# Moving the last x^T phi(k) products: one behind each query product, instead of two in a row at tile 15

## The chip, the cores and the metric

The kernel runs on one core of a Trainium2 chip. The metric is the device time of one execution in microseconds (us), as the median of several runs. TensorE (PE in the profile) does the matmuls, VectorE (DVE) and ScalarE (ACT) take results out of PSUM, GpSimd (POOL) does some elementwise work in SBUF. A profile also gives a span, which is some 1.7 us shorter than the time.

## The reference, cut to what matters

```python
def reference(A_x, A_wqkv, A_wo, B_x, B_w1, B_w3, B_w2, gate_w):
    # x: 2048 tokens x 512, bf16
    g = sigmoid((x * gate_w).sum(-1, keepdims=True))
    # A: linear attention, 32 heads of 16
    phi = lambda t: where(t > 0, t + 1, exp(t)) + 1e-6
    pq, pk = phi(q), phi(k)                       # q, k, v = x @ wqkv
    kv = einsum("bhsd,bhse->bhde", pk, v)         # sum over all tokens
    z  = einsum("bhsd->bhd", pk)                  # sum over all tokens
    a  = (pq . kv / (pq . z + 1e-6)) @ wo
    # B: SwiGLU
    b  = (silu(x @ w1) * (x @ w3)) @ w2
    return g * a + (1 - g) * b
```

The kernel never forms v. It accumulates XP = x^T phi(k), 512 x 512, over the 16 token tiles of 128 tokens (tiles 0 to 15) and gets kv from wv^T XP afterwards. So phase one is: for each tile a product k = x wk, phi(k), and the XP products of an earlier tile. After it come the query products q of the first block of four tiles, the two "remainder" products (the last columns of w1, w3 and the gate), the kv products (kvT), and then the long feed-forward part.

## The kernel before: the parts that matter

phi takes ScalarE once and VectorE twice:

```python
    def phi(dst, ps):
        e_ins = nc.scalar.activation(out=e[:], in_=ps, func=ACT.Exp)
        nc.vector.tensor_scalar(                       # L142, "the min step", bf16 in SBUF
            out=em[:], in0=e[:], scalar1=1.0, scalar2=1e-6, op0=ALU.min, op1=ALU.add)
        nc.vector.scalar_tensor_tensor(                # L145, reads PSUM, writes phi
            out=dst, in0=ps, scalar=0.0, in1=em[:], op0=ALU.max, op1=ALU.add)
```

GpSimd adds up phi(k) of each tile for z (`pks`, L194), and splits the sum into two bf16 parts at the end (`pks_hi` L423, `pks_lo` L425):

```python
    def emit_k_phi(k_ps, t):
        e_ins = phi(pk_sb[:, t, :], k_ps[:])
        ... # t == 0: a copy
            nc.gpsimd.tensor_add(pks[:], pks[:], pk_sb[:, t, :])
```

The XP products of tile t are four matmuls of 128x512 into four PSUM banks. k, q, the remainder products (`emit_rem`) and the feed-forward products share four other banks in turn (pool `psM`), so a product needs the bank that the fourth product before it used.

The order of the PE instructions is that of the program text. The order of the other engines' instructions is set by the scheduler of the framework, and each engine then runs its own list in that order. The order at the end of phase one, before:

```python
    for t in range(TPB, NT):                                   # TPB = 4, NT = 16
        for u in range(n_xp, n_xp + (2 if t in (NT - 4, NT - 1) else 1)):
            emit_xp(u, XP_ps)
            n_xp = u + 1
        emit_k(t)
    emit_q(0, 0, psM, "mm")
    emit_xp(NT - 2, XP_ps)
    emit_q(0, 1, psM, "mm")
    emit_xp(NT - 1, XP_ps)
    for dc in range(KC):                     # the four "XP casts", PSUM to SBUF
        if dc % 2 == 0:
            nc.scalar.activation(out=XP_sb[:, dc, :], in_=XP_ps[dc][:], func=ACT.Copy)
        else:
            nc.vector.tensor_copy(out=XP_sb[:, dc, :], in_=XP_ps[dc][:])
    emit_q(0, 2, psM, "mm")
    emit_q(0, 3, psM, "mm")
    emit_rem(0, 0, psM, "mm")
    emit_rem(0, 1, psM, "mm")
    ... # kvT: reads XP_sb, then the feed-forward part
```

I write k13 for the k product of tile 13, XP13 for its XP products, q0 to q3 for the query products. On PE the order is: k13 XP11 k14 XP12 XP13 k15 q0 XP14 q1 XP15 q2 q3 rem0 rem1 kvT.

## Time and profile before

| | before |
|---|---|
| time, median of the first 3 runs | 180.62 us (180.34 to 180.81) |
| span of the profiled run | 178.7 us |
| PE busy | 174.9 us, 98% |
| granted clock of PE | full in every slice |
| pair of XP products at tile 12 (XP8 and XP9) | 1.73 us |
| pair of XP products at tile 15 (XP12 and XP13) | 1.80 us |

The page, head and the two rows of slices for PE (40 equal slices of the span; a digit is the busy share, or the granted clock, in tenths):

```profile
span 178.7 us, 2488 instructions
PE 174.9 (98%) x893; PEld 84.6 (47%) x893; DVE 118.2 (66%) x205; ACT 66.6 (37%) x126; POOL 61.4 (34%) x69
...
PE   8999999999999999999999999999999999999993
PEclk9999999999999999999999999999999999999999
```

PE is the bound, but its busy share hides small holes, because the ends of matmuls are modelled and overlap the next start: one 128x512 matmul shows 379 ns, but a group of four takes only 0.86 us, 216 ns each. The chain of waits (start, length, what) has a step for each group of matmuls and shows a hole as an overlong step. Here is the chain of before at the end of phase one:

```profile
22.90 1.73 PE XP L204 x8
...
26.36 0.86 PE k_ps L184 x4
27.22 0.86 PE XP L204 x4
28.08 0.86 PE k_ps L184 x4
28.95 1.80 PE XP L204 x8
30.74 0.86 PE k_ps L184 x4
...
35.06 1.73 PE q_ps L217 x8
36.79 1.36 PE r_ps L241 x16
38.15 0.89 PE kvT_ps L413 x16
39.04 0.86 PE gate_ps L310 x4
39.91 0.86 PE up_ps L318 x4
```

Four full matmuls take 0.86 us. Eight take 1.73 us at tile 12 and 1.80 us at tile 15: that 0.07 us is the only irregular step in this stretch. The timeline of all engines (start, length, engine, line, what, idle time before it) shows what it waited for:

```profile
27.64 1.16 POOL L194 TENSOR_TENSOR pks<-pks,pk_sb 128x512 f32<-128x512 f32 x1 [1.02 <-DVE pk_sb L145]
27.89 1.05 DVE L142 TENSOR_SCALAR phi_m<-phi_e 128x512 bf16<-128x512 bf16 x1 [0.39 <-ACT phi_e L140]
...
28.78 1.96 PE L204 MATMUL XP<-pk_sb,x_sb 128*128 128x512 bf16 x8
28.98 0.69 DVE L145 SCALAR_TENSOR_TENSOR pk_sb<-k_ps,phi_m 128x512 bf16<-128x512 f32 x1
...
29.72 0.53 PEld L204 LDWEIGHTS <-x_sb 128*128 128x128 bf16 x3 [0.19 <-issue]
...
35.27 0.28 DVE L142 TENSOR_SCALAR phi_m<-phi_e 128x512 bf16<-128x512 bf16 x1
35.35 1.22 POOL L425 TENSOR_TENSOR pks_lo<-pks,pks_hi 128x512 bf16<-128x512 f32 x1
```

phi of tile 13 is done at 28.98 + 0.69 = 29.67 us; XP13 would have come up at 28.78 + 0.86 = 29.64 us. (From the end of VectorE's work to the start of the matmul that needs it some 0.04 us more pass.) The profile names nothing that the weight loads waited for before 29.72 ("issue"). The min step of tile 13 took 1.05 us, while GpSimd's addition was running. Where it meets no earlier GpSimd instruction it takes 0.28 or 0.29 us, as at 29.61 us for tile 14; the min steps of tiles 11 and 12 met additions too, and took 1.02 and 0.61 us.

### The profile page before, as it was taken

The page shows a single profiled execution, that of the slowest core. Times are in us where ns is not written, and L with a number is a line of the kernel's source. Part 1 is how long each engine was busy: PE and PEld are TensorE (multiplying, and loading weights), DVE is VectorE, ACT ScalarE, POOL GpSimd, SP SyncE. Part 2 cuts the span into 40 slices and gives each one's busy share as a digit, 9 for nine tenths or more (in the row PEclk, how much of TensorE's full clock was granted, in tenths as well). Part 3 has the DMA queues.
Part 4 walks back from the last instruction along what each step waited for, and adds up shares of the span by engine and source line. Part 5 has one row for each costly group of instructions (what it writes and reads, how often), then busy time and mean ns, then how long its engine had stood idle before and what let it go on. Part 6 is the DMA issues. An engine that isn't in the chain of part 4 may idle for free.

```text
span 178.7 us, 2488 instructions
## 1 busy us (share of the span) xinstructions
PE 174.9 (98%) x893; PEld 84.6 (47%) x893; DVE 118.2 (66%) x205; ACT 66.6 (37%) x126; POOL 61.4 (34%) x69
## 2 busy tenths in 40 slices
PE   8999999999999999999999999999999999999993
PEld 3544444474444545444444544444545444444463
DVE  0588867696998837398786375978754669776000
ACT  3642322666533333342433333342433323341221
POOL 5187575646353323262003232620032328100000
PEclk9999999999999999999999999999999999999999
DMA  6999999601005010124000111240001023300011
GB/s 177 265 280 290 298 362 355 216 0 28 9 11 108 0 48 29 44 54 93 0 4 6 38 37 37 59 93 2 0 7 58 15 62 64 61 0 0 29 44 50
DMA packets 29085, 14.88 MB, mean 83 GB/s; under 512 B 19632, under 2 KB 28816, under 8 KB 29072
## 3 DMA queue, kind: packets, MB, share of 16 engines
q1 hardware_dynamic: 28800, 14.46, 29.5%
q10 hardware_dynamic: 272, 0.26, 0.5%
q8 instruction: 7, 0.11, 0.3%
q14 instruction: 6, 0.05, 0.1%
HBM read 8.42 MB, written 2.10 MB: 59 GB/s over the span
## 4 chain that ended last, share of the span: by engine, by line
PE 98%; DVE 0%; issue 0%; DVEq 0%
PE o_ps L355 19%; PE up_ps L318 19%; PE gate_ps L310 19%; PE XP L204 8%; PE o_ps L346 8%; PE q_ps L217 8%; PE k_ps L184 6%; PE r_ps L241 3%; PE k L184 2%; PE o_ps L350 2%; PE warm L161 2%; PE xTp L174 1%; PE kvT_ps L413 1%; PE W_ps L440 0%; DVE o_out L364 0%; PE z_ps L431 0%
## 5 line engine op out<-in xcount | busy, mean ns | idle before, releaser
L318 PE MATMUL up_ps<-xT,w_sb 128*128 128x512 bf16 x160 | 41.1, 379 | 0.0
L310 PE MATMUL gate_ps<-xT,w_sb 128*128 128x512 bf16 x160 | 41.1, 379 | 0.0
L225 POOL TENSOR_TENSOR qz<-pq,z_sb 128x512 f32<-128x512 bf16 x16 | 18.5, 1164 | 60.3 <-DVE pq L145 58.4
L323 ACT ACTIVATE th<-gate_ps 128x512 bf16<-128x512 f32 x40 | 23.9, 597 | 38.1 <-PE gate_ps L310 37.7
L355 PE MATMUL o_ps<-w_sb,hT 128*128 128x512 bf16 (+2 forms) x180 | 37.5, 355 | 0.0
L325 DVE SCALAR_TENSOR_TENSOR gs<-th,gate_ps 128x512 bf16<-128x512 bf16 x40 | 27.4, 684 | 5.8 <-ACT th L323 5.5
L328 DVE TENSOR_TENSOR hT<-up_ps,gs 128x512 bf16<-128x512 f32 x40 | 27.6, 691 | 3.8
L142 DVE TENSOR_SCALAR phi_m<-phi_e 128x512 bf16<-128x512 bf16 x32 | 14.1, 440 | 19.8 <-ACT phi_e L140 19.7
L355 PEld LDWEIGHTS <-hT 128*128 128x128 bf16 x180 | 16.8, 98 | 17.9
L318 PEld LDWEIGHTS <-w_sb 128*128 128x128 bf16 x160 | 15.6, 98 | 18.9
L310 PEld LDWEIGHTS <-w_sb 128*128 128x128 bf16 x160 | 15.6, 98 | 18.7
L360 ACT ACTIVATE o_out<-o_ps,omg 128x512 bf16<-128x512 f32 (+2 forms) x17 | 11.2, 656 | 30.4 <-PE o_ps L355 30.4
L290 POOL TENSOR_TENSOR pqn<-pq,rden 128x512 bf16<-128x512 bf16 x16 | 16.6, 1056 | 14.0 <-DVE rden L283 11.7
L194 POOL TENSOR_TENSOR pks<-pks,pk_sb 128x512 f32<-128x512 f32 x15 | 17.3, 1155 | 8.3 <-DVE pk_sb L145 7.8
L228 DVE TENSOR_REDUCE den<-qz 128x32 f32<-128x512 f32 x16 | 11.0, 685 | 9.0 <-POOL qz L225 8.9
L346 PE MATMUL o_ps<-W_sb,pqT 128*128 128x512 bf16 (+2 forms) x72 | 16.8, 355 | 0.0
L217 PE MATMUL q_ps<-wq_sb,xT 128*128 128x512 bf16 x64 | 16.3, 379 | 0.0
L204 PE MATMUL XP<-pk_sb,x_sb 128*128 128x512 bf16 x64 | 16.2, 379 | 0.0
L140 ACT ACTIVATE phi_e<-k_ps 128x512 bf16<-128x512 f32 x12 | 7.2, 597 | 15.4 <-PE k_ps L184 13.1
L184 PE MATMUL k_ps<-wk_sb,xT 128*128 128x512 bf16 x48 | 12.3, 379 | 0.0
L140 ACT ACTIVATE phi_e<-q_ps 128x512 bf16<-128x512 f32 x16 | 9.6, 597 | 7.0 <-PE q_ps L217 5.8
L145 DVE SCALAR_TENSOR_TENSOR pq<-q_ps,phi_m 128x512 bf16<-128x512 f32 x16 | 11.1, 691 | 0.5
(59 smaller groups left out, 119.3 us busy)
## 6 DMA issues: line engine op xcount, KB each, us to landing
w_sb<-in_B_w_dram SPq DMA_DIRECT2D x6, 640.0 KB, 8.6
out_dram<-o_out SPq DMA_DIRECT2D x15, 128.0 KB, 1.7
x_sb<-in_A_x_dram SPq DMA_DIRECT2D x3, 512.0 KB, 4.0
x_sb<-in_A_x_dram SPq DMA_DIRECT2D x2, 256.0 KB, 3.7
wq_sb<-in_A_wqkv_dram SPq DMA_DIRECT2D x1, 512.0 KB, 5.1
wv_sb<-in_A_wqkv_dram SPq DMA_DIRECT2D x1, 512.0 KB, 6.8
wo_sb<-in_A_wo_dram SPq DMA_DIRECT2D x1, 512.0 KB, 10.0
wk_sb<-in_A_wqkv_dram ACTq DMA_DIRECT2D x1, 256.0 KB, 3.8
```

Source lines behind the costliest of these rows:

```text
L184: nc.tensor.matmul(k_ps[:], lhsT=xT[:, kc, t * P : (t + 1) * P], rhs=wk_sb[:, kc, :], start=(kc == 0), stop=(kc == KC - 1),)
L194: nc.gpsimd.tensor_add(pks[:], pks[:], pk_sb[:, t, :])
L204: nc.tensor.matmul(XP_ps[dc][:], lhsT=x_sb[:, t, dc * P : (dc + 1) * P], rhs=pk_sb[:, t, :], start=(t == 0), stop=(t == NT - 1),)
L217: nc.tensor.matmul(q_ps[:], lhsT=xT[:, kc, ts_tok], rhs=wq_sb[:, kc, :], start=(kc == 0), stop=(kc == KC - 1),)
L225: nc.gpsimd.tensor_tensor(out=qz[:], in0=st[tb, "pq"][:, tt, :], in1=z_sb[:], op=ALU.mult)
L310: nc.tensor.matmul(gate_ps[:], lhsT=w1_sb[:, kc, fsl], rhs=xT[:, kc, tok_sl], start=(kc == 0), stop=(kc == KC - 1),)
L318: nc.tensor.matmul(up_ps[:], lhsT=w3_sb[:, kc, fsl], rhs=xT[:, kc, tok_sl], start=(kc == 0), stop=(kc == KC - 1),)
L323: nc.scalar.activation(out=th[:], in_=gate_ps[:], func=ACT.Tanh, scale=0.5)
L325: nc.vector.scalar_tensor_tensor(out=gs[:], in0=th[:], scalar=1.0, in1=gate_ps[:], op0=ALU.add, op1=ALU.mult)
L328: nc.vector.tensor_tensor(out=st[tb, "hT"][:, fc, :], in0=up_ps[:], in1=gs[:], op=ALU.mult)
L346: nc.tensor.matmul(o_ps[:], lhsT=st[tb, "pqT"][:, c, tsl], rhs=W_sb[:, c, a:b], start=(c == 0), stop=False,)
L355: nc.tensor.matmul(o_ps[:], lhsT=st[tb, "hT"][:, fc, tsl], rhs=w2_sb[:, fc, a:b], start=False, stop=(fc == FC - 1),)
```

## The change

The intent: do not run XP12 and XP13 in a row at tile 15, but give each of the last three tiles' XP products a query product in front of it, so that phi of the tile has time to finish.

```diff
     for t in range(TPB, NT):
-        for u in range(n_xp, n_xp + (2 if t in (NT - 4, NT - 1) else 1)):
+        for u in range(n_xp, n_xp + (2 if t == NT - 4 else 1)):
             emit_xp(u, XP_ps)
             n_xp = u + 1
         emit_k(t)
-    emit_q(0, 0, psM, "mm")
-    emit_xp(NT - 2, XP_ps)
-    emit_q(0, 1, psM, "mm")
-    emit_xp(NT - 1, XP_ps)
+    for tt in range(TPB - 1):
+        emit_q(0, tt, psM, "mm")
+        emit_xp(n_xp + tt, XP_ps)
     ... # the four XP casts, unchanged
-    emit_q(0, 2, psM, "mm")
-    emit_q(0, 3, psM, "mm")
+    emit_q(0, TPB - 1, psM, "mm")
```

The PE order becomes: k13 XP11 k14 XP12 k15 q0 XP13 q1 XP14 q2 XP15 q3 rem0 rem1 kvT. Two things happen: the pair is parted, and XP13 to XP15, with the casts behind the last, move one product later, so k15 and q0 to q2 come one product earlier.

## The prediction

> **What bounds the kernel.** The tensor engine (PE) alone. The page gives PE 98% of a 178.7 us span at full granted clock in every slice; the chain of waits is 98% PE, and the groups table shows no idle time before any of its large matmul groups. As the Trainium skill warns (page "Perfetto Trace Analysis", section "Identifying the Most-Contended Engine"), busy share is a poor measure for PE, since modelled ends overlap: one 128x512 matmul shows 379 ns. So I use the steps of the chain: every four such matmuls take 0.86 us, 216 ns each, the fully streamed rate that the skill's page "TensorE: Matmul & The Clock Gate" gives (section "Back-to-back issue gap"). A change that leaves the matmuls as they are can win only where this stream has a hole.
>
> **What the change removes, adds, moves.** Nothing is added or removed: 64 XP matmuls and 16 of the first block's query matmuls before and after. Only PE order changes. Before: XP12 XP13 k15 q0 XP14 q1 XP15 q2 q3. After: XP12 k15 q0 XP13 q1 XP14 q2 XP15 q3.
>
> **The hole.** The chain shows the pair of XP products at tile 12 taking 1.73 us (full rate) and the pair at tile 15 taking 1.80 us. In the timeline, phi(k) of tile 13 is finished on VectorE at 28.98 + 0.69 = 29.67 us, while XP13 could start at about 28.78 + 0.86 = 29.64 us; weight loads show one idle time of 0.19 us just before 29.72. So the pair loses 0.07 us to phi(k13): its min step on VectorE took 1.05 us instead of 0.29, beside GpSimd's addition of the previous tile. With k15 and q0 in between, XP13 starts near 31.4, 1.7 us after its operand. That hole goes: -0.07 us, all on the critical path.
>
> **What moves against it.** XP15 ends 0.8 us later, so the four XP evacuations end at about 37.0 instead of 36.16 us. Their reader, kvT, started at 37.99, now about 37.92: margin falls from about 1.8 to about 0.9 us. q2 and its phi now compete with those casts on VectorE. Work there from 35 to 39 us is about 4.1 us (three query chains partly, two casts), close to full, but its readers (rem1, gate 0, up 0 through the four PSUM buffers) are needed only at about 37.2, 38.8 and 39.7. Earlier q0 and q1 (by 0.9 us) give some slack back. The new operands are there: phi(k14) ready at 30.63 for an XP14 at 33.1; phi(k15) at an estimated 33.0 for an XP15 at 34.8; the query weights landed at about 19.3 us. GpSimd's sum feeds z at 40.8, with more than 4 us to spare. I expect no new hole; a small chance of 0.1 to 0.5 us at kvT or gate 0.
>
> **Prediction.** 180.62 - 0.07 = 180.55 us; range 180.2 to 180.9, which is mainly the spread of runs (180.34 to 180.81). Chance of faster by over 2%: 0.01; within 2%: 0.98; slower by over 2%: 0.01.
>
> **What the profile would show.** Right: matmul counts unchanged; the XP steps of the last tiles each 0.86 us, no piece of 1.80; the weight load's wait of 0.2 us gone; kvT starting some 0.07 us earlier, with no PE wait on XP_sb; everything after shifted by 0.07 us; span near 178.6. Wrong: a PE or weight-load idle before kvT (XP_sb late), before the first gate/up matmuls (a PSUM buffer late), or before XP15 (phi(k15) late behind GpSimd's addition).
>
> **What would make it wrong.** The automatic order of VectorE and ScalarE work placing the query phi before the XP casts, so that kvT waits; or another meeting of the min step with GpSimd delaying a buffer; or a change of allocation that moves later stages. Each is of a few tenths of a microsecond, well below 2%.

## The result

| | before | after |
|---|---|---|
| time, median of 6 runs | 180.47 us (180.28 to 180.81) | 180.35 us (180.26 to 181.01) |
| ratio, with 95% interval | | 0.9998 (0.998 to 1.0015): the same |
| span of the profiled run | 178.7 us | 178.7 us |
| from the start of k13 to the first up product | 39.91 - 26.36 = 13.55 us | 39.89 - 26.41 = 13.48 us |

A ratio is the mean time of one kernel's fast runs over the mean of the other's of the same rounds, so it is not quite the ratio of the medians.

The page of after. 16 matmul records are missing from its trace (877 against 893; the weight loads are complete, 893 in both, and the edit only changes the order of calls), which is why PE shows 97%:

```profile
span 178.7 us, 2472 instructions
PE 174.1 (97%) x877; PEld 84.6 (47%) x893; DVE 119.3 (67%) x205; ACT 66.6 (37%) x126; POOL 61.3 (34%) x69
```

The chain of after, the same stretch. Two "issue" pieces of 0.05 us, in the lines left out, stand where a record is missing; the starts of the next groups show that no time is lost there:

```profile
26.41 0.86 PE k_ps L184 x4
27.27 0.86 PE XP L204 x4
28.13 0.86 PE k_ps L184 x4
29.00 0.86 PE XP L204 x4
29.86 0.86 PE k_ps L184 x4
30.72 0.86 PE q_ps L217 x4
31.59 0.86 PE XP L204 x4
...
36.77 1.36 PE r_ps L241 x16
38.13 0.89 PE kvT_ps L411 x16
...
39.89 0.86 PE up_ps L318 x4
```

The step of 1.80 us is gone: every group takes 0.86 us. Between k13 and the first up product there are twelve groups of four, 1.36 us of remainder, 0.89 us of kvT and 0.86 us of gate. In before, 23 such groups in a row took 28.95 - 9.09 = 19.86 us, 0.8635 us each; so the sum is 10.36 + 3.11 = 13.47 us, within rounding of the 13.48 us that after needs. No hole is left in this stretch, so at this pace of the matmuls no reordering of it can give more. The 13.55 us of before rests on one profile, the figure of after on two (after and e9).

The timeline of after, the engines that take the results away:

```profile
35.18 1.16 POOL L423 TENSOR_TENSOR pks_lo<-pks,pks_hi 128x512 bf16<-128x512 f32 x1
35.51 0.69 DVE L402 CAST XP_sb<-XP 128x512 bf16<-128x512 f32 x1 [0.21 <-PE XP L204]
...
36.12 0.37 DVE L142 TENSOR_SCALAR phi_m<-phi_e 128x512 bf16<-128x512 bf16 x1
...
36.41 0.68 DVE L402 CAST XP_sb<-XP 128x512 bf16<-128x512 f32 x1
```

The last XP cast ends at 36.41 + 0.68 = 37.09 us, 0.88 us before kvT starts at 37.97 us in the PE timeline.

The 0.07 us does not show in the span, for a plain reason: in the chain, k13 of after starts 0.05 us later than that of before, ahead of anything that the change touches. In the profiled runs below that start lies anywhere between 25.85 and 26.94 us. So all small verdicts below are read from the stretch k13 to first up, which leaves that jitter out.

### The profile page after: what moved, and what is told of

It reads as the page before. It is cut to its first block, busy times and chain, and to the rows that moved or that the text cites. A ratio compares the mean times of both kernels' runs of the same rounds, so it can differ in the third digit from the quotient of the medians.

```text
span 178.7 us, 2472 instructions
## 1 busy us (share of the span) xinstructions
PE 174.1 (97%) x877; PEld 84.6 (47%) x893; DVE 119.3 (67%) x205; ACT 66.6 (37%) x126; POOL 61.3 (34%) x69
## 4 chain that ended last, share of the span: by engine, by line
PE 97%; issue 1%; DVE 0%; DVEq 0%
PE o_ps L355 19%; PE gate_ps L310 19%; PE up_ps L318 19%; PE o_ps L346 8%; PE q_ps L217 8%; PE XP L204 8%; PE k_ps L184 6%; PE r_ps L241 3%; PE k L184 2%; PE o_ps L350 2%; PE warm L161 2%; PE xTp L174 1%; PE kvT_ps L411 1%; PE W_ps L438 0%; DVE o_out L364 0%
## 5 line engine op out<-in xcount | busy, mean ns | idle before, releaser
L318 PE MATMUL up_ps<-xT,w_sb 128*128 128x512 bf16 x156 | 40.5, 379 | 0.2
L142 DVE TENSOR_SCALAR phi_m<-phi_e 128x512 bf16<-128x512 bf16 x32 | 15.2, 475 | 18.9 <-ACT phi_e L140 18.8
```

Of the source, the lines that this page charges most:

```text
L318: nc.tensor.matmul(up_ps[:], lhsT=w3_sb[:, kc, fsl], rhs=xT[:, kc, tok_sl], start=(kc == 0), stop=(kc == KC - 1),)
```

## The experiments

The theory: PE is one stream without holes, except where an operand or a bank is late; the 0.07 us was a wait for phi of tile 13; that phi was late because its min step met GpSimd's addition. The rivals: that two XP groups in a row cost something by themselves or that 0.07 us is an artefact of modelled ends; and that moving XP15 later costs, or gives back, part of the gain.

"k13 to up" is the stretch of the chain of waits in each profiled run.

| run | PE order or other edit | k13 to up | against before | ratio of times (95%) |
|---|---|---|---|---|
| before | | 13.55 | 0 | 1 |
| after | the change | 13.48 | -0.07 | 0.9998 (0.998 to 1.0015) |
| e9 | the change again | 13.49 | -0.06 | 1.0006 (0.9984 to 1.0028) |
| e1 | XP13 before XP12 | 14.41 | +0.86 | 1.0058 (1.0039 to 1.0078) |
| e2 | XP13 amid XP12 | 13.98 | +0.43 | 1.0028 (1.0007 to 1.005) |
| e3 | e1, GpSimd addition moved | 13.66 | +0.11 | 1.0001 (0.9983 to 1.0018) |
| e4 | before, GpSimd addition moved | 13.48 | -0.07 | 0.9985 (0.9967 to 1.0003) |
| e5 | pair parted by k15 alone | 13.92 | +0.37 | 1.0029 (1.0003 to 1.0056) |
| e10 | e5 without the `pks_lo` subtraction | 13.48 | -0.07 | 0.9999 (0.9982 to 1.0016) |
| e11 | the change, XP15 behind q3 | 14.59 | +1.04 | 1.007 (1.0049 to 1.009) |
| e6 | the same kernel as e11 | no usable profile | | 1.0073 (1.0047 to 1.0099) |
| e8 | the change, XP15 just before kvT | 15.34 | +1.79 | 1.0105 (1.0081 to 1.013) |

### e1 and e2: make the wait larger

The same instructions as before, in another order. e1 runs XP13 ahead of XP12; e2 puts XP13 between the two halves of XP12.

```diff
-            emit_xp(u, XP_ps)
+            emit_xp({12: 13, 13: 12}.get(u, u), XP_ps)      # e1
```
```diff
+            if u == NT - 4: emit_xp(u, XP_ps, (0, 1))        # e2 (chunks 0, 1)
+            else:           emit_xp(u, XP_ps)
+            if u == NT - 3: emit_xp(u - 1, XP_ps, (2, 3))
```

> The kernel before with the pair at tile 15 in the other order, XP13 then XP12. Theory (PE waits for phi of tile 13, ready at about 29.67 us): XP13 comes up 0.86 us earlier, so the hole grows from 0.07 to about 0.93 us and the time by about 0.86 us, to ratio about 1.0048. Rival (the 0.07 us is a cost of two XP groups in a row, or an artefact of modelled ends, not a wait for an operand): pair still near 1.80 us, time unchanged.

> The kernel before with XP13 in the middle of XP12 (chunks 0 and 1, then XP13, then chunks 2 and 3). Theory: hole about 0.5 us, time longer by about 0.43 us, ratio about 1.0024, halfway between before and e1. Rival: unchanged.

Measured: +0.86 us and +0.43 us in the stretch, as expected to 0.01 us. In time, e1 took 181.69 us against 180.46 us; its ratio is 1.05 us, with an interval of 0.70 to 1.41 us, and e2's is 0.51 us (0.13 to 0.90). The chain of e1 now runs through phi of tile 13:

```profile
26.94 0.88 PE k_ps L184 x4
...
27.84 0.61 ACT phi_e L140
...
28.46 1.06 DVE phi_m L142
...
29.55 0.70 DVE pk_sb L145
30.25 0.04 issue
30.30 1.89 PE XP L204 x8
```

The wait grows by what the products in front of XP13 lose. It is a wait for an operand, not a price of two groups in a row and not an artefact: the device time moves with it.

### e3 and e4: take away GpSimd's addition

GpSimd's addition of tile 12 is moved behind that of tile 13, so that it cannot run beside the min step of tile 13. PE's order is that of e1 in e3, and that of before in e4.

```diff
-        else:
+        elif t != NT - 4:
             nc.gpsimd.tensor_add(pks[:], pks[:], pk_sb[:, t, :])
+        if t == NT - 3:
+            nc.gpsimd.tensor_add(pks[:], pks[:], pk_sb[:, NT - 4, :])
```

> e1 with GpSimd's addition of tile 12 to the sum pks moved behind that of tile 13, so that nothing runs on GpSimd beside the min step of tile 13. Theory (the min step took 1.05 instead of 0.29 us because of that addition): phi of tile 13 is ready 0.76 us earlier, the hole of e1 shrinks from about 0.93 to about 0.15 us, time within 0.1 us of before. Rival (the min step is slow for another reason): as e1, about 0.86 us longer than before.

> The kernel before, its PE order kept, with GpSimd's addition of tile 12 moved behind that of tile 13. Theory: min step of tile 13 about 0.29 us, the pair at tile 15 at the full 1.73 us, the wait of the weight load gone, span 0.07 us less without any change of PE order; time not told from before (0.07 us is under the noise of about 0.3 us). Rival (pair cost): still 1.80 us.

Measured: e3 is 0.11 us longer than before in the stretch and 1.0001 in time, where e1, with the same PE order, is 0.86 us longer. So 0.75 of e1's 0.86 us came from the meeting with GpSimd. e4 gains the 0.07 us with PE's order unchanged. Its timeline, the min step of tile 13 and the pair:

```profile
27.71 0.29 DVE L142 TENSOR_SCALAR phi_m<-phi_e 128x512 bf16<-128x512 bf16 x1 [0.46 <-ACT phi_e L140]
...
28.60 1.89 PE L206 MATMUL XP<-pk_sb,x_sb 128*128 128x512 bf16 x8
```

The min step takes 0.29 instead of 1.05 us, and the pair 1.89 instead of 1.96 us. So the hole of before could also be closed on GpSimd, and two XP groups in a row run at the full rate. e4's ratio of 0.9985 has an interval that includes 1; the trace accounts for 0.07 us, which is 0.0004, and no more is claimed.

This is where the Trainium skill helps to read the trace: "SBUF — State Buffer", section "Who interferes with whom", says that GpSimd and a VectorE instruction of the kind that may use two ports take turns on a shared port pair, and that whoever comes second is blocked completely, not slowed. This trace agrees: in before GpSimd's addition ends at 27.64 + 1.16 = 28.80 us and the min step at 27.89 + 1.05 = 28.94 us, 0.14 us behind it, though it needs 0.28 us alone. The two min steps before it started 0.28 and 0.70 us into an addition and ended 0.15 and 0.16 us behind it (addition 24.44, min step 24.59 us; addition 26.61, min step 26.77 us). So what sets the end is the end of the other instruction.

### e9: the change again

> The changed kernel again, for a tighter interval. Theory: 0.07 us less than before, ratio 0.9996, which the noise will not show; the trace from the start of the XP product after k14 to the first gate matmul 0.07 us shorter than in before. Rival (gained back later): this stretch equal to that of before.

Measured: 180.33 us against 180.04 us, ratio 1.0006. As expected, the noise of the runs does not show 0.07 us; the stretch does, with 13.49 us.

### e5 and e10: part the pair, but leave XP15 where it was

In e5, k15 alone parts the pair: XP12 k15 XP13 q0 XP14 q1 XP15 q2 q3.

```diff
-        for u in range(n_xp, n_xp + (2 if t in (NT - 4, NT - 1) else 1)):
+        for u in range(n_xp, n_xp + (2 if t == NT - 4 else 1)):
...
+    emit_xp(NT - 3, XP_ps)
     emit_q(0, 0, psM, "mm")
     emit_xp(NT - 2, XP_ps)
```

> Half of the change: XP12 k15 XP13 q0 XP14 q1 XP15 q2 q3, so the pair is parted by k15 alone and XP15 stays where it was in before. Theory: hole gone (XP13 comes up at about 30.5 us, 0.8 us after its operand), stretch as in the full change, margin of kvT about 1.8 us as in before. Rival (moving XP15 later costs something): faster than the full change in the trace.

Both expectations missed. e5 has no hole at XP13, but it is 0.44 us longer than the change in the stretch, and 0.37 us longer than before. Its timeline shows a new wait at the second remainder product:

```profile
34.88 0.69 DVE L404 CAST XP_sb<-XP 128x512 bf16<-128x512 f32 x1 [0.51 <-PE XP L204]
...
35.41 1.16 POOL L426 TENSOR_TENSOR pks_lo<-pks,pks_hi 128x512 bf16<-128x512 f32 x1
35.48 1.23 DVE L142 TENSOR_SCALAR phi_m<-phi_e 128x512 bf16<-128x512 bf16 x1
...
37.23 0.67 DVE L145 SCALAR_TENSOR_TENSOR pq<-q_ps,phi_m 128x512 bf16<-128x512 f32 x1
...
37.96 0.84 PE L241 MATMUL r_ps<-wr_sb,xT 128*128 128x193 bf16 x8 [0.28 <-DVE pq L145]
```

The min step of q1 came 0.07 us after GpSimd's `pks_lo` subtraction had started, and took 1.23 us. So q1's bank came free late, and rem1, the fourth product after q1, waited for it. In before, the lines shown above have the same two instructions the other way round: the min step at 35.27 us, `pks_lo` at 35.35 us. Before had won this race by 0.08 us. In e5 k15 comes earlier, so GpSimd's sum is ready earlier, and the race is lost.

e10 takes the suspect away: `pks_lo` is a constant zero, written at the start. Its result is slightly less exact.

```diff
+    pks_lo = consts.tile([P, D], BF16, name="pks_lo")   # ahead of phase one
+    nc.gpsimd.memset(pks_lo[:], 0.0)
...
-    nc.gpsimd.tensor_sub(pks_lo[:], pks[:], pks_hi[:])
```

> e5 with one suspected cause taken away: the GpSimd subtraction that makes pks_lo (1.16 us, at 35.41 us in e5) is replaced by a constant zero written at the start, on purpose a slightly less exact result. Theory (in e5 the min step of q1 took 1.23 instead of 0.28 us because it met that subtraction, so a PSUM buffer came free late and the second remainder tile waited): min step 0.28 to 0.4 us, no wait before the second remainder tile, stretch from k of tile 13 to the first up product 13.48 us as in the changed kernel, against 13.92 in e5; ratio about 0.9996. Rival (XP15 too early crowds VectorE by itself): the hole of about 0.45 us stays, ratio about 1.002.

Measured: 13.48 us, no wait at rem1, and the min step of q1 at its usual length:

```profile
35.36 0.28 DVE L144 TENSOR_SCALAR phi_m<-phi_e 128x512 bf16<-128x512 bf16 x1
```

So the meeting with `pks_lo` was the whole of e5's 0.44 us. Moving XP15 later, which I had taken for a cost of the change, keeps the change out of this trap: in after, `pks_lo` (35.18 us) falls beside an XP cast from PSUM, and only the last piece of it meets a min step (0.37 us at 36.12). The min step of q1, which comes one product earlier there, had started at 33.98 us, ahead of `pks_lo`.

### e6, e11 and e8: how much room is left behind XP15

e6 and e11 are one kernel: the change with XP15, and the casts, behind q3. e8 has them right before kvT.

```diff
     for tt in range(TPB - 1):
         emit_q(0, tt, psM, "mm")
-        emit_xp(n_xp + tt, XP_ps)
+        if tt < TPB - 2:
+            emit_xp(n_xp + tt, XP_ps)
     emit_q(0, TPB - 1, psM, "mm")
+    ... # e8 only: emit_rem(0, 0), emit_rem(0, 1) here
+    emit_xp(NT - 1, XP_ps)
+    ... # the four XP casts here
```

> The changed kernel with XP15 one more product later, behind q3. Theory (margin of kvT in the changed kernel is 0.88 us: kvT 37.97, last XP cast ended 37.09): XP casts end about 0.86 us later, near 37.95, hole at kvT 0 to 0.1 us, time unchanged. Rival (XP casts wait for the queue of query work, so the margin is an illusion): hole of 0.3 us or more.

> The changed kernel with XP15 right before kvT. Theory: XP15 starts near 37.1, the last cast ends about 2.2 us later as in the changed kernel, near 39.3, or somewhat later behind the work of the two remainder tiles; kvT could start at 37.97, so a hole of about 1.2 to 1.5 us, time longer by the same, ratio about 1.007. Rival (XP15's place is free): unchanged.

The profile of e6 fell in an execution of 1058.74 us. It is of no use here and is left out of every comparison. The other five runs of e6 took 181.23 to 181.96 us, ratio 1.0073 (1.0047 to 1.0099): not unchanged, so the expectation failed. e11 is the same kernel, for a usable profile:

> e6 again, whose profile fell in an execution of 1057 us. Its timed runs were 1.3 us longer than before, not equal. Theory now (VectorE takes the XP casts of its in-order list between and behind the phi steps of q2 and q3): last cast near 38.5 to 39.0 us, kvT waits for it 0.6 to 1.2 us, ratio about 1.005 to 1.007. Rival (a PSUM buffer that comes late): the hole stands before a remainder tile, the first gate or the first up product.

Measured: 181.37 us against 180.16 us, and 1.11 us more than the change in the stretch, as now expected. The timeline of e11:

```profile
34.84 1.16 POOL L425 TENSOR_TENSOR pks_lo<-pks,pks_hi 128x512 bf16<-128x512 f32 x1
...
35.38 0.77 DVE L142 TENSOR_SCALAR phi_m<-phi_e 128x512 bf16<-128x512 bf16 x1 [0.41 <-ACT phi_e L140]
...
36.99 0.69 DVE L405 CAST XP_sb<-XP 128x512 bf16<-128x512 f32 x1
37.59 0.68 DVE L145 SCALAR_TENSOR_TENSOR pq<-q_ps,phi_m 128x512 bf16<-128x512 f32 x1
38.19 0.68 DVE L405 CAST XP_sb<-XP 128x512 bf16<-128x512 f32 x1
...
38.92 0.89 PE L413 MATMUL kvT_ps<-XP_sb,wv_sb 128*128 128x128 bf16 x13 [0.92 <-DVE XP_sb L405]
```

kvT waits for the last XP cast, which VectorE's list has behind the whole phi of q2 and of q3; in after only the min step of q2 stood between the two casts and nothing of q3 ahead of them. XP15 starts at 35.41 us in this PE timeline, so the last cast ends 3.46 us after it; in after it was 37.09 - 34.88 = 2.21 us. In e8 the casts stand behind the remainder's work as well, and its stretch is 1.86 us longer than that of the change, where I had expected 1.2 to 1.5 us. The direction was right, the size too small: I had kept the 2.2 us fixed, and in e8 it was 2.84 us (XP15 at 36.55, last cast ended at 39.39).

The order of the list is not the only cause here. The min step of q2 (35.38 us in e11) met `pks_lo`, which ended at 36.00 us, and took 0.77 us instead of 0.28; it lies on the chain that ended in kvT. So, as an estimate from these lengths, some 0.49 of e11's 1.11 us belongs to that meeting and some 0.6 us to the order. The same min step took 0.73 us in e8. No run has XP15 behind q3 without `pks_lo`, so the shares are not shown.

## Why the prediction was right

- **The bound.** Right. The stretch in question holds 13.48 us of gapless matmuls, and after takes 13.48 us.
- **The hole of 0.07 us and its disappearance.** Right: 1.80 us for the pair before, 0.86 us for every group after, stretch 0.07 us shorter (0.06 in e9). e1 and e2 scaled the wait to 0.86 and 0.43 us above before, e3 took 0.75 us of it away again.
- **Its cause.** Right: the min step beside GpSimd's addition. e4 closed the same hole with PE's order untouched.
- **No new hole.** Right for the change itself: the XP casts ended at 37.09 us, predicted about 37.0, and kvT did not wait. phi of tile 15 was ready at 33.13 us in after, estimated 33.0; its min step now met GpSimd's additions and took 1.01 us instead of 0.29, which cost nothing, because XP15 came only at 34.88. That no query phi met `pks_lo` at a bad place was partly luck: the prediction named such a meeting as a risk, but did not look where `pks_lo` would fall, and before had escaped it by 0.08 us.
- **The time.** 180.35 us measured, 180.55 predicted, within the range. This agreement carries little: the spread of runs is 0.5 us and more, and the 0.07 us was only ever to be seen in the trace. The span did not fall to 178.6 us, as I had expected, because k13 of that run started 0.05 us later.
- **What was judged wrongly without hurting the number.** I booked the later place of XP15 only as something "against" the change, with a margin of 0.9 us. e11 shows that the margin is not there to spend: one product (0.86 us) later costs 1.11 us, because VectorE's list changes with the place (phi of q3 moves in front of and between the casts) and because the min step of q2 meets `pks_lo`, in shares that no run separates. And e5 with e10 shows that XP15 staying where it was would have cost 0.44 us by the meeting with `pks_lo`. Of the four places of XP15 tried with the pair parted and `pks_lo` in its place (e5, the change, e11, e8), the one the change chose is the only one without a hole.

No version tried beats both kernels by more than the noise. e4 and the change each reach the floor of this stretch, 13.48 us (so does e10, with a less exact result).

## What to carry to other kernels

When one engine's stream is 98% full, look for overlong steps in its chain of waits: their sum is all that a reordering of that stretch can win, here 0.07 of 180 us. A "margin" between a producer's end and its consumer's start holds only while the in-order lists of the engines between them, and what these meet on the way, stay the same; here moving a product by one place changed both, and cost 1.11 us where the margin promised 0 to 0.1. And where VectorE and GpSimd share work, whether a short bf16 step takes 0.28 or 1.23 us turned here on 0.15 us of order (0.08 us ahead of `pks_lo` in before, 0.07 us behind it in e5), so part a pair or move a group only with both engines' timelines in view.

## What the Trainium skill lacked or had wrong

- "TensorE: Matmul & The Clock Gate", section "Back-to-back issue gap": it gives about 131 ns per matmul for a sustained stream of weight load and matmul pairs at N=512, and calls about 216 ns the isolated case. An earlier section of the same page ("Step-by-step: what each phase is for") gives 216 ns as the back-to-back gap, so the page contradicts itself. In this kernel, where every matmul has its own weight load, the stream takes 0.86 us for four, 216 ns each, from 9.09 us to the end of phase one; no group of four such matmuls in the chain of before is faster.
- "SBUF — State Buffer", section "Who interferes with whom": right that the second comer is fully blocked. It gives no time from the other's end to the blocked instruction's end: the min step, 0.28 us alone, ended 0.14 us after GpSimd's instruction (before: 28.80 and 28.94 us; e5: 36.57 and 36.71 us).
- "TensorE: Matmul & The Clock Gate", section "Seeing it yourself", warns that recorded clock events can be unreliable and that the clock has been seen stuck at a quarter for over 50 us. No page that was searched describes an execution like the first of e6: a span of 1057.0 us with a recorded granted clock of 1.0, in which the 128x512 matmuls took 1.70 us each instead of 0.38 and started 1.32 us apart instead of 0.216, about six times slower, while VectorE and ScalarE were busy for 110 and 67 us (118 and 67 in before). It did not come again in five further runs of e6 or in six of the same kernel as e11. Its cause stays open.
